# A decode-attention gradient kernel: K and V loads issued when four slots are free instead of three

## The chip, the cores and the metric

The kernel runs on one core of a Trainium2 chip. The metric is device microseconds for one execution: from three runs of the kernel before, a median of 731.6 us (lowest 729.88, highest 732.12).

## What is computed

The reference is one decode step (one token, width 640) of a layer with attention and a gated MLP side by side, forward and backward:

```python
xn = _layernorm(x)
# A: 32 heads of 128, each with its own K and V cache of 8192 x 128, bfloat16
q = (xn @ wq) ; scores = q k^T * 128**-0.5 ; p = softmax(scores) ; o = p v ; attention = o @ wo
# B: silu(xn @ w1) * (xn @ w3) @ w2, with 1728 hidden columns
out = x + attention + B
return out, and the gradients of <out, grad_out> for x, k_cache, v_cache, wq, wo, w1, w3, w2
```

With one query row, the gradients of the caches are outer products: dV is the softmax row times the gradient of o, dK is the gradient of the scores times q. So for each head the kernel reads K (2 MB) and V (2 MB) and writes dK (2 MB) and dV (2 MB). The page counts 151.34 MB read and 151.34 MB written.

## The kernel before

**Tiles and slots.** K or V of one head is one SBUF tile of 128 partitions x 8192 bfloat16 values, 2048 KB. There are ten such tiles (`NSLOT = 10`), named `kv` in the profile whatever they hold; the list `free_slots` is a first-in, first-out list of the free ones. Nothing is computed into a second tile: the outer products dV and dK are written by VectorE over the V and K that they belong to (L466), and the slot is stored to HBM from there.

**The order on the queue.** The schedule is written by hand. All K and V loads and all dK and dV stores are issued by SyncE (SP in the profile) through `fifo` (L105), in the order in which the program reaches them; SP waits in front of each one until what it needs is done, and everything behind it on SP waits too. Loads go K0, V0, K1, V1, ... and stores V0, K0, V1, K1, ... Each store is followed by an attempt to load:

```python
def load_next():
    if not pending or len(free_slots) < lag[0]:
        return
    ...
def store(kind, h):
    ...
    fifo((dkc if kind == "K" else dvc)[h], t[:])
    free_slots.append(t)
    load_next()
```

A slot counts as free in the program as soon as its store is issued. The load that takes it must wait on the chip until that store has landed. With `lag[0]` at 3, a load that follows a store takes the slot of the store two places earlier in the queue.

**The first heads.** Six loads (K0, V0, K1, V1, K2, V2) go out with `lag[0]` at 1; the other four slots (`mA` to `mD`) hold the MLP weights. Then `lag[0]` is set for the rest of the program (L160). Heads 0 and 1 follow; their stores are V0, K0, V1, K1. The MLP is computed ahead of head 2 (`MLP_AT = 2`), with its own stores issued by GpSimd (POOL); as each of its four slots is given back, `load_next` is tried again (L632, L666, L677).

**One head.** `head(h)` transposes K and V in eight pieces each (`T`, L318 on TensorE, L320 on ScalarE), multiplies them with q and with the gradient of o (`Mp`, L339), makes the softmax (`expo`, `zsum`, `probs`), and sums over K and V (`wsum`, L433). The outer products of head h-1 are made inside head h: `outers_a(h - 1)` at its start (all of dV with its store, half of dK), `outers_b(h - 1)` after `probs(h)` (the other half of dK, and its store). TensorE's first pieces of K of the next head are transposed before a head ends.

**Groups and the end.** Every four heads the weights wq and wo of a group are loaded by GpSimd and their gradients are stored, mostly by GpSimd. After head 31 come the last outer products, the gradients of the last group (`fin_wo` L520, `fin_wq` L526 and L528; their stores are split in two and go by SP, L515), and the input gradient (L843 to L865). Four small stores of the two output rows are issued by ScalarE (L849, L867). SP's last store of dwq waits until one of these small stores has landed.

Of the kernel before, what the change touches and what calls it, by code (L numbers as in the profile page):

```python
# [21 lines left out]
def kernel(  # L22
# [97 lines left out]
    lag = [1]  # L120
# [36 lines left out]
    for _ in range(2):  # L157
        load_next()

    lag[0] = 3  # L160

    ident_f = consts.tile([P, P], F32, name="ident_f")
    make_identity(nc, ident_f[:])
# [734 lines left out]
```

## Time and profile before

| what | value |
|---|---|
| median of the runs | 731.6 us |
| span of the profiled execution | 727.5 us |
| around the span (median less span; the page gives no other total of that execution) | 4.1 us |
| moved by DMA | 303.54 MB, 417 GB/s over the span |
| TensorE matmul busy | 603.3 us (83%) |
| VectorE busy | 459.8 us (63%) |
| ScalarE busy | 376.2 us (52%) |
| GpSimd busy | 32.3 us (4%) |

Busy times are sums over one execution and overlap each other. The DMA figures are a mean over the core's 16 DMA engines; a transfer of a K or V tile is spread over all 16 in 128 packets of 16 KB, and it has landed when the last engine is done with its share. The chain of work that ended last is followed back from the last instruction, and its shares say what was waited for, not what was busy.

### The profile page before, as it was taken

The page shows a single profiled execution, that of the slowest core. Times are in us where ns is not written, and L with a number is a line of the kernel's source. Part 1 is how long each engine was busy: PE and PEld are TensorE (multiplying, and loading weights), DVE is VectorE, ACT ScalarE, POOL GpSimd, SP SyncE. Part 2 cuts the span into 40 slices and gives each one's busy share as a digit, 9 for nine tenths or more (in the row PEclk, how much of TensorE's full clock was granted, in tenths as well). Part 3 has the DMA queues.
Part 4 walks back from the last instruction along what each step waited for, and adds up shares of the span by engine and source line. Part 5 has one row for each costly group of instructions (what it writes and reads, how often), then busy time and mean ns, then how long its engine had stood idle before and what let it go on. Part 6 is the DMA issues. An engine that isn't in the chain of part 4 may idle for free.

```text
span 727.5 us, 12942 instructions
## 1 busy us (share of the span) xinstructions
PE 603.3 (83%) x5186; PEld 377.1 (52%) x5193; DVE 459.8 (63%) x811; ACT 376.2 (52%) x727; POOL 32.3 (4%) x48
## 2 busy tenths in 40 slices
PE   4989489999899989888897789878796988988930
PEld 2547366665565556555454456445554555545510
DVE  4169646688868776667565756457665666667581
ACT  3640746665666566545454546455463555655510
POOL 0010100000000000000010000000000000000000
PEclk9997799999999999989998989899998999999965
DMA  9999999999999999999999999999999999999995
GB/s 351 400 411 421 428 426 430 427 426 430 420 420 431 430 412 420 426 428 421 420 425 428 430 426 428 420 431 428 421 422 427 429 425 423 425 432 427 426 415 221
DMA packets 28625, 303.54 MB, mean 417 GB/s; under 512 B 3354, under 2 KB 5929, under 8 KB 11924
## 3 DMA queue, kind: packets, MB, share of 16 engines
q1 hardware_dynamic: 22578, 277.75, 90.5%
q0 software_dynamic: 5968, 24.94, 8.5%
q8 instruction: 41, 0.67, 0.4%
q14 instruction: 20, 0.16, 0.1%
q10 hardware_dynamic: 18, 0.01, 0.0%
HBM read 151.34 MB, written 151.34 MB: 416 GB/s over the span
## 4 chain that ended last, share of the span: by engine, by line
DMA 51%; PE 36%; DVE 7%; ACT 2%; issue 1%; SPq 0%; ACTq 0%; DVEq 0%
DMA kv<-in_A_v_cache_dram 20%; PE pT L318 17%; DMA out_dram<-kv 16%; DMA kv<-in_A_k_cache_dram 14%; PE sA L339 5%; PE dA L339 4%; PE X L433 3%; DVE kv L466 3%; PE m L356 2%; DMA wo_g<-in_A_wo_dram 2%; ACT KT L320 1%; PE gu_ps L561 1%; PE pT L266 1%; PE m L400 1%; ACT KT L346 0%
## 5 line engine op out<-in xcount | busy, mean ns | idle before, releaser
L320 ACT COPY KT<-pT 128x512 f32<-128x512 f32 x512 | 288.3, 588 | 227.9 <-PE pT L318 208.6
L318 PE MATMUL pT<-ident_f,kv 128*128 128x128 f32 x2048 | 308.2, 290 | 53.7 <-DMA kv<-in_A_v_cache_dram 24.2
L318 PEld LDWEIGHTS pT<-ident_f,kv 128*128 128x128 f32 x2048 | 237.4, 149 | 146.2 <-PE pT L318 51.8
L466 DVE TENSOR_TENSOR kv<-qd,U 128x4096 bf16<-128x4096 bf16 x64 | 146.0, 2284 | 0.0
L466 DVE TENSOR_TENSOR kv<-qd,P 128x4096 bf16<-128x4096 bf16 x64 | 143.6, 2285 | 0.0
L433 PE MATMUL X<-kv,Z 128*32 128x512 bf16 x1024 | 97.1, 413 | 1.8 <-DVE Z L450 1.8
L339 PE MATMUL dA<-KT,qz 128*32 128x512 bf16 x512 | 84.2, 408 | 0.0
L339 PE MATMUL sA<-KT,qz 128*32 128x512 bf16 x512 | 83.5, 406 | 0.0
L416 DVE SCALAR_TENSOR_TENSOR U<-m,P 128x64 bf16<-128x64 f32 x32 | 7.5, 233 | 87.4 <-PE m L356 87.4
L433 PEld LDWEIGHTS <-Z 128*32 128x32 bf16 x1024 | 33.2, 101 | 35.3 <-issue 8.7
L339 PEld LDWEIGHTS <-qz 128*32 128x32 bf16 x1024 | 29.5, 95 | 40.8 <-issue 38.3
L382 DVE TENSOR_REDUCE mrow<-m 128x1 f32<-128x64 f32 x32 | 7.1, 223 | 68.4 <-PE m L356 68.3
L356 PE MATMUL m<-selc,KT 64*128 64x64 f32 x256 | 30.5, 242 | 10.3 <-ACT KT L346 10.3
L356 PEld LDWEIGHTS m<-selc,KT 64*128 64x128 f32 x256 | 21.5, 144 | 33.2 <-ACT KT L346 22.1
L376 ACT CAST qd<-pT 128x256 bf16<-128x256 f32 x32 | 11.9, 372 | 39.9 <-DVE kv L466 28.7
L389 DVE TENSOR_REDUCE negM<-m 128x1 f32<-128x128 f32 x32 | 9.3, 292 | 33.0 <-PE m L386 33.0
L526 DVE SCALAR_TENSOR_TENSOR wq_g<-wq_g,side 128x512 bf16<-128x512 bf16 x40 | 27.3, 683 | 0.0
L257 DVE SCALAR_TENSOR_TENSOR side<-wo_g,g_bc 128x640 bf16<-128x640 bf16 x32 | 26.2, 819 | 1.3 <-DMA wo_g<-in_A_wo_dram 0.9
L448 DVE SCALAR_TENSOR_TENSOR U<-m,P 128x128 bf16<-128x128 f32 x32 | 11.4, 356 | 16.3 <-PE m L446 16.3
L406 DVE RECIPROCAL rZ<-m 128x1 f32<-128x1 f32 x32 | 5.3, 166 | 24.2 <-PE m L400 24.2
L346 ACT COPY KT<-dA 64x512 f32<-64x512 f32 x32 | 18.6, 582 | 3.7 <-PE dA L339 3.7
L346 ACT COPY KT<-sA 64x512 f32<-64x512 f32 x32 | 18.6, 581 | 2.1 <-PE sA L339 1.9
(162 smaller groups left out, 372.7 us busy)
## 6 DMA issues: line engine op xcount, KB each, us to landing
out_dram<-kv SPq DMA_DIRECT2D x64, 2048.0 KB
kv<-in_A_k_cache_dram SPq DMA_DIRECT2D x32, 2048.0 KB
kv<-in_A_v_cache_dram SPq DMA_DIRECT2D x32, 2048.0 KB
wq_g<-in_A_wq_dram POOLq DMA_DIRECT2D x7, 640.0 KB, 13.4
wo_g<-in_A_wo_dram POOLq DMA_DIRECT2D x7, 640.0 KB, 19.1
out_dram<-wo_g POOLq DMA_DIRECT2D x7, 640.0 KB, 14.4
kv<-in_B_w_dram SPq DMA_DIRECT2D x2, 1728.0 KB
out_dram<-kv POOLq DMA_DIRECT2D x2, 1728.0 KB, 23.5
```

The costliest lines, as they stand in the source:

```text
L257: nc.vector.scalar_tensor_tensor(junk[:], G_["wo"][:, hh, :], 1.0, g_bc[:], ALU.mult, ALU.mult, accum_out=G_["do"][:, hh:hh + 1])
L318: nc.tensor.transpose(pT[:, k * P:(k + 1) * P], W3[:, 4 * c + k, :], ident_f[:])
L320: nc.scalar.copy(KT[:].rearrange("p k w -> p (k w)"), pT[:])
L339: nc.tensor.matmul(S_[kind][q:q + QW, :], lhsT=S_["qz"][:, o:o + QW], rhs=KTb[c][:, par, :], start=(c0 == 0 and par == 0), stop=(c0 == NCH ...
L346: nc.scalar.copy(XS[0:QH].rearrange("p k w -> p (k w)"), S_.pop(kind)[0:QH, :])
L356: nc.tensor.matmul(S_["m"][:, b0:b0 + 4 * J].rearrange("p (x c k t) -> p k x c t", x=4, k=4, t=2)[:, k], lhsT=XS[0:QH, k, :], rhs=selc[0:Q ...
L376: nc.scalar.copy(qd[:].rearrange("p a d -> p (a d)"), hd[h].pop("ps_r"))
L389: nc.vector.tensor_reduce(S_["negM"][:], S_["m"][:, 2 * J:2 * J + P], AX.X, ALU.max, negate=True)
L433: nc.tensor.matmul(xg["X"][q:q + QW, :], lhsT=Z[:, o:o + QW], rhs=W[:, N4 * i:N4 * (i + 1)], start=(slot == 0 and i < 4), stop=(slot == NS ...
L448: nc.vector.scalar_tensor_tensor(S_["U2"][:], S_["V"][:, 0:J].unsqueeze(2).to_broadcast([P, J, 2]), S_["m"][:, OC + NS:OC + NS + 1], S_["P ...
L466: nc.vector.tensor_tensor(dst[:, lo * DH:hi * DH].rearrange("p (j a b) -> p j a b", a=DH // 2, b=2), vec.rearrange("p (a b) -> p a b", b=2 ...
L526: nc.vector.scalar_tensor_tensor(wq_g[:, ci, :], wq_g[:, ci, :], 1.0, dqb, ALU.mult, ALU.mult, accum_out=dxa[:, ci, g:g + 1])
```

## The change

After the six first loads, `load_next` asks for four free slots instead of three.

```diff
     for _ in range(2):
         load_next()
 
-    lag[0] = 3
+    lag[0] = 4
```

The instructions of TensorE, VectorE, ScalarE and GpSimd stay as they are, in the same order. On SP the same 148 rows stand in another order. K3 no longer precedes the store of K1 but follows it; V3, K4, V4 and K5 follow it as before; V5 no longer precedes the store of V2 but follows it; and every later load stands behind one store more than before. The last load, V31, stood between the stores of K27 and V28 and now stands between those of V28 and K28. A load that follows a store takes the slot of the store three places earlier in the queue instead of two.

## The prediction

> **What bounds the kernel now.** I read the page's slices first, then stretches of the span, SP's own waits and issues, and the chain at the end. The slices show no stage after the first in which the transfers rest:
>
> ```profile
> DMA  9999999999999999999999999999999999999995
> GB/s 351 400 411 421 428 426 430 427 426 430 420 420 431 430 412 420 426 428 421 420 425 428 430 426 428 420 431 428 421 422 427 429 425 423 425 432 427 426 415 221
> ```
>
> Stretches (start and end, length, busy time of PE, weight loads, DVE, ACT and POOL, then granted clock, busy share of the DMA engines, GB/s) show the same where this change acts:
>
> ```profile
> 110.00:120.00 10.00, 10.00 (x100) 6.25 (x100) 6.29 (x12) 6.01 (x13) 0.00 (x0) 1.00 1.01 430
> 120.00:130.00 10.00, 9.41 (x76) 5.89 (x74) 8.62 (x17) 6.90 (x16) 0.00 (x0) 1.00 1.00 424
> ...
> 300.00:657.00 357.00, 303.98 (x2511) 187.25 (x2515) 219.47 (x370) 187.80 (x373) 14.60 (x18) 0.92 1.01 426
> ...
> 690.00:700.00 10.00, 5.13 (x55) 2.64 (x54) 9.27 (x10) 1.92 (x5) 0.00 (x0) 0.85 0.99 419
> 700.00:705.00 5.00, 1.81 (x12) 0.88 (x12) 3.88 (x8) 0.59 (x1) 0.00 (x0) 0.50 0.95 403
> 705.00:710.00 5.00, 0.00 (x0) 0.00 (x0) 4.82 (x17) 0.00 (x0) 0.00 (x0) 0.50 1.00 426
> 710.00:715.00 5.00, 0.93 (x3) 0.59 (x3) 2.24 (x12) 0.00 (x0) 0.00 (x0) 0.50 0.82 325
> 715.00:720.00 5.00, 0.00 (x0) 0.00 (x0) 0.00 (x0) 0.00 (x0) 0.00 (x0) 0.50 0.80 284
> 720.00:727.50 7.50, 0.00 (x0) 0.00 (x0) 0.00 (x0) 0.00 (x0) 0.00 (x0) 0.50 0.26 92
> ```
>
> All 16 DMA engines are busy from 10 us to about 690 us, and still mostly busy after the last outer product. PE is not the bound: 304 of 357 us in the long middle stretch. So the kernel runs at the rate of its transfers, and the order of two transfers in the queue costs time only where an engine of the 16 runs out of work. SP's waits look alarming, and are only the other face of this:
>
> ```profile
> SPq L105 <- DMA out_dram<-kv: 470.8, 55, 14.7
> SPq L105 <- DVE kv L466: 83.4, 13, 12.9
> ```
>
> SP stands 471 us in front of loads whose slot is still being stored; while it stands, up to four earlier transfers are under way.
>
> **The change part by part.** No byte, no instruction of an engine and no duration changes: a 2.097 MB tile at the 426 GB/s of the middle stretch is 4.92 us of all 16 engines, before and after. What moves is each load's place, by one store.
>
> *The middle, 130 to 650 us.* The load into a slot waits for the store three places back, not two, so up to six transfers may be under way instead of four. SP's wait moves to the stores. For the second half of dK of head h, VectorE needs `probs(h+1)`, and that comes behind pieces of V(h+1) on TensorE. At the end of the trace V31 lands at 683.3 and VectorE begins that half of dK30 at 690.2, done at 692.5: 9.2 us after the landing. With the new order the load of V(h+1) stands two transfers ahead of the store whose landing releases SP, so SP comes to the store of dK(h) about 4.9 us after V(h+1) landed and waits some 4.3 us for VectorE. Behind that wait stand only loads. What covers it is the queue: seven transfers (34 us of work) were issued behind the landed one. They do not finish evenly: the completion events of the load V31 run from 665.4 on the fastest of the 16 engines to 683.3 on the slowest, 18 us, which leaves the fastest engine about 16 us of work. I cost the middle at 0. Without that cover the 4.3 us would recur per head, some 25 times.
>
> PE's waits for loads (46.7 us in all on L318 in the trace) stay as many: K and V arrive one store later, but at the same rate. Here the Trainium skill speaks against the change: "DMA: Bandwidth & Descriptors", section "Rules for kernel authors", says to issue a DMA early and wait on it late. By that rule a later load is a loss, and taken at its word for V31 it makes the sum 4.9 us longer; in the middle, the rows above say that bytes alone set the pace. The same page's "Specifications" give about 358 GB/s as a core's limit for HBM; the trace holds 426 for 357 us, so the measurement decides, and by the page one tile would be an estimated 5.9 us.
>
> *Behind the MLP, 92 to 130 us.* Here a store moves ahead of a load where VectorE is late. SP's issues before:
>
> ```profile
> 92.75 0.96 SPq L105 DMA_DIRECT2D kv<-in_A_k_cache_dram  x1
> 107.20 0.33 SPq L105 DMA_DIRECT2D kv<-in_A_v_cache_dram  x1
> 120.41 0.34 SPq L105 DMA_DIRECT2D out_dram<-kv  x1
> 124.47 0.33 SPq L105 DMA_DIRECT2D kv<-in_A_k_cache_dram  x1
> 129.68 0.34 SPq L105 DMA_DIRECT2D out_dram<-kv  x1
> ```
>
> The load at 107.20 is V5; the store at 120.41 is dV2, which waited 12.9 us for VectorE (the longest of the waits on L466). After the change V5 stands behind dV2 and is issued at about 120.8. Until then the engines live on K5 and on POOL's MLP stores, the last of which was issued at 98.3 and landed 29.7 us later, at 128.0. dV2 landed between 128.6 and 132.2 on the 16 engines, median 130.1; less its own 4.9 us, the engines were free for it at 123.7 to 127.3, median 125.2. Without V5 they are free 4.9 us sooner: 118.8 to 122.4, median 120.3. A transfer issued at 120.4 reaches the engines about 1 us later (a store of dwo at the end: issued 709.14, first packet 710.10). So the fastest engine rests 2.6 us, the median one 1.1 us, the slowest not at all. The end is set by engines that are late, so the cost lies between 0 and 2.6 us; I take 0.6, nearer to the slow ones. The next pair then comes at 129.7 instead of a load at 124.5 and a store at 129.7; dV2 and V5 keep the engines until 131.2 or later, and the new packets start at 130.7. No second gap, but a margin of only 0.5 us.
>
> *Before that, 57 to 92 us,* dK1 is issued when VectorE is done with it (61.6 us; the row of its outer product starts at 57.12 and lasts 4.49) instead of at 66.71 behind K3. The engines are full in both orders, and K3 is needed only from about 98 us: 0.
>
> *The end.* This is the place where the later load can show. The chain of waits there:
>
> ```profile
> 657.53 25.79 DMA kv<-in_A_v_cache_dram
> ...
> 698.30 4.48 DVE kv L466 x2
> ...
> 713.40 0.28 DVE fin_bf L865
> ```
>
> V31 lands at 683.3; dK31 is done 19.5 us later at 702.8, and the last result of all, `fin_bf`, at 713.7. With one more store ahead of it, V31 lands 4.9 us later, at 688.2, and all of that chain moves by 4.9: dV31 done at 703.3, dK31 at 707.7, `fin_bf` at 718.6. Does the end move? The completion events of the last stores on the slowest engine follow at 4.9 to 6.3 us without a break: 709.1, 713.9, 718.7 and for dK31 723.6. There dK31, issued at 704.3, did not start before 718.7: 14.4 us of slack, of which the change uses 3.4. The two pieces of the slowest engine behind it (dwo, dwq) need their data by 710.2 and 715.2 instead of 705.3 and 710.3, still ahead of 723.6. What does depend on the chain is SP's last store, 340 KB of dwq on few engines, issued at 721.1 when ScalarE's small store of `fin_bf` had landed. That one was issued at 713.7 and its packets ran only at 719.4 to 720.6, behind the dwo part that was issued at 712.1. After the change the dwo part is issued at about 717.1. Its 272 packets (68 partitions, four rows each) are 55 ns each and run on four engines, 68 on each, 3.7 us: from 718 to 722. Then `fin_bf` has landed between 719.9 and 722.2, and the last store goes out between 1.1 us sooner and 1.1 us later than now. I take +0.4; if it keeps its present distance to `fin_bf`, all 4.9.
>
> **Sum.** 0 + 0.6 + 0 + 0 + 0.4 = +1.0 us: a span of 728.5 against 727.5. The runs' median stands 4.1 us above the span, so 732.6 against 731.6.
>
> **Rivals.**
> - *The end is not covered (slower).* ScalarE's last small store runs 7.4 us after its issue, as now, so that SP's last store is issued at 726.0 and the end moves by the whole 4.9 us. With the 0.6 of the gap: 737.1. It decides if the delay of the small store belongs to its issue and not to the dwo part ahead of it; for it speaks that SP's wait for it is 5.4 us long now, against it that its packets ran beside the last of that part. A part of it is enough for a slowdown from 2 us on.
> - *The gap behind the MLP is whole (slower).* If the engines that rest at 119 us are those that end last, or VectorE brings dV2 or dK2 later, up to one load's worth is lost: 4.9 + 0.4, 736.9. Against it: the backlog of 3.3 to 6.9 us behind 120.4.
> - *A deeper queue feeds the engines better (faster).* If the middle has small rests that six transfers in flight fill, it may rise from 426 to the 430 of the best slices: 1% of 357 us, 3.4 us, less the 1.0: 729.2, or 728.2 without the losses. Against it: the busy share there is 1.01.
> - *Nothing of it acts.* SP's rows do change order and the waits with them, so this would mean only that all is hidden: 731.6, inside the likeliest case.
>
> **How the numbers follow.** A difference of 0.3% (2.2 us) is about what a measurement of this kernel can tell from no change. The covered case is the likeliest, with 0.62: its gap of 0 to 2.6 and its end of -1.1 to +1.1 make -1.1 to +3.7, 730.5 to 735.3; of the 0.62, 0.10 lies above +2.2. The uncovered end has 0.22, the whole gap 0.06, the better-fed engines 0.10. So faster 0.10, same 0.52, slower 0.10 + 0.22 + 0.06 = 0.38. Leaving out the faster rival and what both slower ones together would cost, the range is 729.6 to 737.1.
>
> **What would show it.** In the changed profile: a middle stretch at 425 to 427 GB/s; V5 issued at 120.8; SP waiting far longer for L466 than 83 us and less for stores; a short dip of the DMA share at 119 to 122 us; V31 landing near 688; SP's last store near 721 to 722. I am wrong if V31 lands more than 7 us later (the gap was whole, or the middle slowed), if the middle changes its rate, or if the last store is issued near 726.

## The result, and the profile after

The changed kernel takes 737.91 us (median of 4 runs, 736.33 to 738.78) against 731.4 for the kernel before on the same chip (4 runs): a ratio of 1.0096, with an interval of 1.0077 to 1.0114. A second measurement with other runs of both gave 737.19 against 730.57, 1.0096 again (1.007 to 1.0122). The medians differ by 6.5 us (7.0 by the ratio), where +1.0 was forecast, and the time lies just above the range.

The profiled execution of the changed kernel has a span of 735.7 us and a time of 737.54, so 1.8 us lie around the span. The execution of the kernel before that the prediction was summed on, 727.5 us of span, was thus a quick one, some 2 us below its median; of the 8.2 us between the two spans, about 2 are this choice of executions.

The slices of the page now show a stage in which the transfers rest (the seventh, 110 to 129 us, where the busy share falls one tenth and the rate by a quarter), and behind it a slow slice at 129 to 147 us (396 GB/s) in which the engines are busy:

```profile
DMA  9999998999999999999999999999999999999995
GB/s 355 399 409 423 429 430 322 396 424 422 419 415 428 430 412 425 423 430 425 426 423 428 428 424 421 423 428 430 421 424 422 429 426 415 429 426 429 427 399 205
```

Stretches of the same profile, with the columns as in the prediction (the last three are granted clock, DMA busy share and GB/s):

```profile
110.00:115.00 5.00, 5.00 (x41) 3.19 (x37) 1.96 (x8) 3.78 (x9) 0.00 (x0) 1.00 1.00 423
115.00:120.00 5.00, 5.00 (x60) 2.91 (x59) 2.41 (x5) 2.57 (x5) 0.00 (x0) 1.00 0.87 363
120.00:125.00 5.00, 5.00 (x41) 3.17 (x40) 5.00 (x4) 3.63 (x7) 0.00 (x0) 1.00 0.40 166
125.00:130.00 5.00, 5.00 (x39) 3.09 (x37) 3.69 (x13) 3.30 (x8) 0.00 (x0) 1.00 0.97 347
...
140.00:145.00 5.00, 5.00 (x41) 3.14 (x40) 3.02 (x3) 3.72 (x8) 0.00 (x0) 1.00 1.00 360
...
300.00:657.00 357.00, 302.47 (x2532) 184.38 (x2533) 219.74 (x359) 187.46 (x370) 15.02 (x19) 0.93 1.01 425
...
720.00:730.00 10.00, 0.93 (x3) 0.59 (x3) 3.14 (x15) 0.00 (x0) 0.00 (x0) 0.50 0.66 231
```

Three things are to be seen. At 115 to 130 us the engines rest for 0.13 x 5 + 0.60 x 5 + 0.03 x 5 = 3.8 us; the packet records of 100 to 150 us give 3.96 us of rest per engine, and 0.0 before. At 140 to 145 us the engines are fully busy and still move only 360 GB/s. The middle is what it was: 425 against 426.

SP's issues (start, us, what) say why the engines rest, and where the end lies:

```profile
91.12 0.33 SPq L105 DMA_DIRECT2D kv<-in_A_k_cache_dram  x1
122.81 0.34 SPq L105 DMA_DIRECT2D out_dram<-kv  x1
123.25 0.58 SPq L105 DMA_DIRECT2D kv<-in_A_v_cache_dram  x1
132.07 0.34 SPq L105 DMA_DIRECT2D out_dram<-kv  x1
...
716.28 3.04 SPq L105 DMA_DIRECT2D out_dram<-wo_g  x2
727.42 0.71 SPq L105 DMA_DIRECT2D out_dram<-wq_g  x2
```

After K5 at 91.12 SP issues nothing for 31 us. dV2 comes at 122.81, behind VectorE, and V5 behind it at 123.25 instead of 107.20. K5 has landed by 118.0 and the last store of the MLP between 118.9 and 121.6 on the 16 engines, and dV2's packets begin 0.84 us after its issue. SP's waits show the same stand as the longest one on L466 (total, times, longest):

```profile
SPq L105 <- DMA out_dram<-kv: 234.4, 48, 9.6
SPq L105 <- DVE kv L466: 222.3, 35, 31.3
```

The chain at the end (start, us, what):

```profile
658.89 35.36 DMA kv<-in_A_v_cache_dram
...
709.23 4.49 DVE kv L466 x2
...
724.33 0.28 DVE fin_bf L865
```

V31 lands at 694.25 instead of 683.3, 10.9 us later: the one store of 4.9, and 6.0 from upstream. The whole chain behind it moves by as much; `fin_bf` is done at 724.6. On the slowest engine the transfers are less late: dK31 ends there at 728.7 instead of 723.6, 5.1 us (on the quickest at 720.4 instead of 710.4, 10.0 us). But the two last dwq stores on SP, whose data were ready at 721.2, are issued at 727.42 and 727.80, and the last of them lands at 734.8. In front of them SP waits for ScalarE's small stores of the row `out_0` (tile `KT` in the profile; first what SP waited for, then ScalarE's issues):

```profile
SPq L105 <- DMA out_dram<-KT: 8.0, 1, 8.0
...
721.98 2.67 ACTq L849 DMA_DIRECT2D out_dram<-KT  x2
```

These small stores and the dwq stores behind them use the same two completion semaphores in the trace.

### The profile page after: what moved, and what is told of

Read it like the earlier page. It is cut to its first block, busy times and chain, and to the rows that moved or that the text cites. A ratio compares the mean times of both kernels' runs of the same rounds, so it can differ in the third digit from the quotient of the medians.

```text
span 735.7 us, 12948 instructions
## 1 busy us (share of the span) xinstructions
PE 605.8 (82%) x5193; PEld 376.8 (51%) x5193; DVE 459.7 (62%) x811; ACT 376.5 (51%) x727; POOL 32.3 (4%) x48
## 4 chain that ended last, share of the span: by engine, by line
DMA 53%; PE 33%; DVE 8%; ACT 3%; issue 1%; SPq 0%; ACTq 0%; DVEq 0%
DMA kv<-in_A_v_cache_dram 20%; DMA kv<-in_A_k_cache_dram 16%; PE pT L318 16%; DMA out_dram<-kv 15%; PE sA L339 4%; DVE kv L466 4%; PE dA L339 3%; PE X L433 3%; PE m L356 2%; DMA wo_g<-in_A_wo_dram 2%; ACT kv L642 1%; ACT KT L320 1%; PE gu_ps L561 1%; PE dh_ps L572 1%; PE dx_acc L660 1%
## 5 line engine op out<-in xcount | busy, mean ns | idle before, releaser
L318 PE MATMUL pT<-ident_f,kv 128*128 128x128 f32 x2048 | 305.8, 288 | 65.0 <-DMA kv<-in_A_k_cache_dram 41.5
L318 PEld LDWEIGHTS pT<-ident_f,kv 128*128 128x128 f32 x2048 | 235.2, 148 | 157.5 <-issue 59.7
L466 DVE TENSOR_TENSOR kv<-qd,U 128x4096 bf16<-128x4096 bf16 x64 | 146.0, 2284 | 0.0
L466 DVE TENSOR_TENSOR kv<-qd,P 128x4096 bf16<-128x4096 bf16 x64 | 143.6, 2284 | 0.0
L433 PE MATMUL X<-kv,Z 128*32 128x512 bf16 x1024 | 100.9, 426 | 1.8 <-DVE Z L450 1.8
```

Source lines behind the costliest of these rows:

```text
L318: nc.tensor.transpose(pT[:, k * P:(k + 1) * P], W3[:, 4 * c + k, :], ident_f[:])
L433: nc.tensor.matmul(xg["X"][q:q + QW, :], lhsT=Z[:, o:o + QW], rhs=W[:, N4 * i:N4 * (i + 1)], start=(slot == 0 and i < 4), stop=(slot == NS ...
L466: nc.vector.tensor_tensor(dst[:, lo * DH:hi * DH].rearrange("p (j a b) -> p j a b", a=DH // 2, b=2), vec.rearrange("p (a b) -> p a b", b=2 ...
```

## The experiments

**Theory A (two places).** The main cost is the gap behind the MLP: the engines run dry because V5 stands behind dV2, and dV2 waits for VectorE. A smaller one is the end, where V31 comes one store later. **Theory B:** nearly all of it is the end; the gap is made up by late engines as the prediction had it. **Theory C:** the deeper queue costs something per head. The middle's 425 GB/s already spoke against C.

**1. Only the end.** The three slots stay until head 16; from there it is four.

```diff
     for h in range(H):
+        if h == 16:
+            lag[0] = 4
```

> Four free slots are asked for only from head 16 on; up to there three, as before. V5 keeps its place ahead of dV2, V31 stands behind one store more. Theory A (the engines ran dry behind the MLP, and that is most of the 6.5 us; the end adds some 1 to 3): +1 to +3 us against the kernel before, V31 landing about 4.9 us later than the 683 of before, no dip of the DMA share near 120 us. Theory B (the later last load is what costs, at the end): +5 to +7 us. Theory C (the middle runs slower with loads issued later): about half, +3 to +4, with a rate under 425 GB/s after 360 us only.

Measured: 732.35 us against 730.76 (12 and 24 runs), ratio 1.0019 (1.0002 to 1.0037): 1.4 us by the ratio. No rest at 100 to 150 us (0.01 us). The middle from head 16 on and the end together are worth about a fifth of the loss, so C and B both fall as the main cause. Its last two dwq stores show the same wait as in the changed kernel: VectorE is done with them at 717.2, and SP issues them at 723.1.

```profile
723.10 0.71 SPq L105 DMA_DIRECT2D out_dram<-wq_g  x2
```

**2. Only the gap.** Four slots until head 16, then three and one load more, so that V31 stands where it stood before.

```diff
-    lag[0] = 3
+    lag[0] = 4
...
+        if h == 16:
+            lag[0] = 3
+            load_next()
```

> Four free slots up to head 16, then three again, with one extra load issued there, so that V31 stands where it stood before. Theory A: +4.5 to +6 us, the dip of the DMA share near 120 us as with the change. Theory B: 0 to +1 us. Theory C: +3 to +4 us.

Measured: 735.2 us (7 runs) against 730.76, ratio 1.0055 (1.0034 to 1.0075): 4.0 us, the larger part, a little under the 4.5 to 6 expected. The profiled execution was the quickest of its seven (731.16, span 729.4), and it shows why they spread. There dV2 was issued at 118.87 instead of 122.81, and the rest is almost gone:

```profile
115.00:120.00 5.00, 5.00 (x48) 3.06 (x42) 5.00 (x3) 2.56 (x5) 0.00 (x0) 1.00 0.97 398
120.00:125.00 5.00, 5.00 (x40) 3.14 (x37) 3.79 (x8) 3.95 (x10) 0.00 (x0) 1.00 1.02 394
...
135.00:140.00 5.00, 5.00 (x42) 3.69 (x40) 3.87 (x2) 3.40 (x7) 0.00 (x0) 1.00 1.02 387
```

0.34 us of rest per engine, and yet 387 GB/s at full share: packets took longer here too (see the last section).

**3. The end's wait for the small stores.** The four small stores of the output rows go by GpSimd instead of ScalarE; once with the change (rows4), once with the kernel before (rows3).

```diff
-        nc.scalar.dma_start(out_0v[e:e + 1], ...)
+        nc.gpsimd.dma_start(out_0v[e:e + 1], ...)
...
-        nc.scalar.dma_start(out_1.rearrange(...)[lo:hi, :], fin_bf[lo:hi, :])
+        nc.gpsimd.dma_start(out_1.rearrange(...)[lo:hi, :], fin_bf[lo:hi, :])
```

> The change as it is (four slots throughout), but the four small stores of the two output rows at the end are issued by GpSimd instead of ScalarE, so that SP's last stores of dwq don't share their completion semaphores. If SP's wait for these small stores carries the end (the two dwq stores issued at 727.4 and 727.8 in the changed profile, dwq data being ready at 721.2): the dwq stores go out at 720 to 722, the end follows the slowest engine's dK31 (728.7) by about 3 us, and the time is 2.5 to 4 us below the changed kernel, +2.5 to +4 us against before. If the end follows the engines' backlog alone: as the changed kernel, +6 to +7.

> The kernel before, with the four small stores of the output rows issued by GpSimd. If the wait for them carries the end of the kernel before too (last dwq store issued at 721.1, data ready at 710.3): 1 to 2 us faster than before. If the slowest engine's dK31, landed at 723.6, sets the end there: within 0.5 us of before.

Measured: rows4 734.6 us, ratio 1.0056 (1.004 to 1.0072); rows3 729.09, ratio 0.9975 (0.9959 to 0.999), both against 730.76. In rows4 SP issues the two dwq stores when VectorE has made them, not 6 us later:

```profile
720.80 2.67 SPq L105 DMA_DIRECT2D out_dram<-wq_g  x2
```

So the wait for the small stores costs about 3 us in the changed kernel (737.2 and 737.9, less 734.6; by the ratios, 1.0096 less 1.0056, 2.9 us) and 1.7 us in the kernel before. Some 1 to 1.5 us of the change's loss go through that wait; 5.5 us between rows4 and rows3 do not, and the rest of 3.55 us behind the MLP is still there in rows4.

**4. dV2 earlier.** In the MLP the products of w3 over blocks of 256 columns, and their sums into the input gradient, are left out (line 654 runs over w1 alone), so that VectorE and TensorE are done with the MLP sooner; the kernel leaves out that part of the input gradient. Once with the change (less4), once without (less3).

```diff
-            for f0 in range(0, F, FA):
+            for f0 in range(0, F if wi == 0 else 0, FA):
```

> The changed kernel (four slots), with one piece of the MLP left out: of the input gradient's sum over w3 the part over the first four column blocks (seven products on VectorE, their sums on TensorE) isn't computed, which takes some 5 us of VectorE out of the stretch ahead of dV2. The transfers stay as they are. Theory A (the engines run dry because dV2, which now stands in front of V5, waits for compute): dV2 is issued at 116 to 118 us instead of 122.8, the engines run dry for 0 to 1 us instead of about 4, and the time is about that of the same kernel with three slots plus what the end costs: +1 to +2.5 us over that one. Without theory A: +6 us over that one, as before.

> The kernel before (three slots) with the same piece of the MLP left out. The engines are full around 120 us, so less compute there buys nothing: within 1 us of before. If compute ahead of head 3 sets the time: 4 to 5 us faster.

Measured: less4 732.54 us, ratio 1.0032 (1.002 to 1.0043); less3 729.46, ratio 0.9985 (0.9973 to 0.9997), against 730.18 (21 runs). In less4, dV2 and V5 are issued 6.4 us earlier than in the changed kernel:

```profile
116.36 0.34 SPq L105 DMA_DIRECT2D out_dram<-kv  x1
116.81 1.19 SPq L105 DMA_DIRECT2D kv<-in_A_v_cache_dram  x1
```

The rest is 0.01 us, packets keep their length, and the slowest engine ends dK31 at 723.1, where it did before. Between the two kernels with the shorter MLP the change costs 3.1 us, instead of 6.5. So with the gap closed, what is left is the end; it is larger here than the 1.4 us of late4 and than the 1 to 2.5 expected, with intervals that just meet. SP's last store of dwq is issued at 724.05 in less4 and at 720.96 in less3, 3.1 us later, as much as the time: in less4 the loss passes through the wait for the small stores.

**5. One slot more, one slot less.** If a place in the queue is what counts, five slots must be worse again, and two must move loads ahead.

```diff
-    lag[0] = 3
+    lag[0] = 5     (lag5)
+    lag[0] = 2     (lagtwo)
```

> Five free slots instead of three: K5 too stands behind dV2 (V5 behind dK2), and V31 two stores later than before. Theory A: the engines have one load less still and run dry for 8 to 9 us before dV2 arrives, with slower packets after it; with the end +11 to +16 us. Theory B or C (the later last load, the smaller lead alone, in proportion): about twice the change, +11 to +14, but without a longer dip near 120 us.

> Two free slots instead of three: every load one store earlier, V31 between the stores of V27 and K27; a load waits for the store just ahead of the last one, so only some three transfers are under way. If engines run dry in the middle because fast engines catch up with so short a queue: slower than before, +2 to +10 us, with a share under 1.00 from 300 to 657 us. If the queue of three is enough: the end gains, 0 to 2 us faster. SP's K6 now stands in front of dV2 and waits for an MLP store until about 124.5 us, which may add a gap of its own.

Measured: lag5 743.92 us, ratio 1.019 (1.0169 to 1.0212); lagtwo 733.48, ratio 1.0052 (1.0032 to 1.0071), against 730.18. In lag5 the engines stand still for nearly five microseconds, 6.0 us of rest in all, and its middle runs at 426 GB/s:

```profile
115.00:120.00 5.00, 5.00 (x48) 2.76 (x47) 4.96 (x5) 2.96 (x6) 0.00 (x0) 1.00 0.06 22
```

The rest is shorter than the 8 to 9 us expected. Rest and longer packets make about 8 of its 13.7 us. At 657 us its packets have moved what the kernel before had moved 8.4 us sooner, and its span ends 13.7 us later, so the remainder arises at the end, where V31 lands at 700.5, 17.2 us later; how it arises there was not followed further. lagtwo is slower too, mostly in the same stage but by another wait:

```profile
125.34 0.33 SPq L105 DMA_DIRECT2D kv<-in_A_k_cache_dram  x1
125.72 0.42 SPq L105 DMA_DIRECT2D out_dram<-kv  x1
```

Now K6 stands ahead of dV2 and waits until a store of the MLP has landed in its slot, so dV2, which VectorE had finished at 120.05, goes out at 125.7; the engines rest 1.5 us. Its middle moves 424 GB/s instead of 426, about 1.5 us in 357 us, with the busy share still at 1.01. In the stage behind the MLP three slots are right because V5 is ahead of dV2 and K6 behind it.

**6. The change behind the MLP, or from head 16 on, with the rows on GpSimd.** rowspost4 sets four slots from head 3 on, so that V5 stays ahead of dV2; rowslate4 does it from head 16; rows3b repeats rows3 beside them.

```diff
+        if h == 3:      (rowspost4; 16 in rowslate4; absent in rows3b)
+            lag[0] = 4
...
-        nc.scalar.dma_start(...)      (the small stores, as in 3)
+        nc.gpsimd.dma_start(...)
```

> Four free slots from head 3 on, that is just behind the MLP: V5 keeps its place ahead of dV2, and K6 and every later load stands behind one store more, as with the change. The small stores of the output rows are issued by GpSimd. So the middle runs with the changed order, and the two places that theory A names are both repaired. Theory A: as the three-slot kernel with the rows on GpSimd, within 2 us (-1.7 to +0.5 us against before); a small rest near 130 us may cost up to 1.5 us, since K6 now follows dK2. If the later loads cost anything in the middle, or V31's later landing at the end by itself: +3 to +6 us over that kernel.

> Four free slots from head 16 on, small stores of the output rows issued by GpSimd. The end alone, with its wait removed: 0 to +0.5 us over the three-slot kernel with the rows on GpSimd if SP's wait for the small stores is the end's whole price; +1.5 to +3 us over it if V31's later landing delays the end in another way.

> The three-slot kernel with the rows on GpSimd once more, as the comparison on the same chip: -1.7 us against before, between -3 and -0.5.

Measured, against 730.93 (25 runs): rowspost4 733.26, ratio 1.0044 (1.0026 to 1.0062); rowslate4 730.89, ratio 1.0012 (0.9994 to 1.003); rows3b 729.29, ratio 0.998 (0.9964 to 0.9996). rowspost4 is 4.0 us slower than rows3b, where theory A had at most 2 us and a costly middle or end +3 to +6; its profile says where:

```profile
119.96 9.63 SPq L105 DMA_DIRECT2D out_dram<-kv  x2
129.63 0.43 SPq L105 DMA_DIRECT2D kv<-in_A_k_cache_dram  x1
```

dV2 finds V5 ahead of it, but the next store, dK2 at 129.25, now stands ahead of K6 at 129.63, where K6 stood at 124.47 before. The gap has moved by one pair: 0.67 us of rest, and again longer packets. It is not the middle: compared with the kernel before at the same bytes moved, the profile is 2.8 us late at 165 us and 2.9 us at 300 and again at 657 us. rowslate4 is 1.6 us slower than rows3b although the small stores hold nothing up: at 690 to 700 us its engines have too little to do (rowslate4 first, then rows3b):

```profile
690.00:700.00 10.00, 9.72 (x73) 5.40 (x71) 3.60 (x8) 5.86 (x12) 0.00 (x0) 0.84 0.75 320
```

```profile
690.00:700.00 10.00, 5.49 (x54) 3.17 (x48) 9.30 (x8) 1.68 (x4) 0.00 (x0) 0.78 0.98 419
```

The stores of dV31 and dK31 cannot be made before V31 is there (it lands at 688.9 in rowslate4 and at 683.0 in rows3b), and no load is left to fill that time. The intervals of the two ratios meet, so the 1.6 us agree with late4's 1.4 and are no sharper than these.

**7. The change again.** The changed kernel a second time.

```diff
-    lag[0] = 3
+    lag[0] = 4
```

> The changed kernel once more, for a second profile and more runs. Theory A, with the engines free for dV2 at 119 to 122 us whatever the run, and dV2 issued between 118.9 and 122.8 us by the clock that TensorE was granted: +5 to +7.5 us in the median, runs spread over 3 us or more, and a dip whose length goes with the issue of dV2 in this profile (about 4 us of rest at 122.8, under 1 us below 119.5). If the dip has another cause, its length doesn't follow that time.

Measured: 737.19 us (6 runs, 737.01 to 739.08), the ratio given above. Its profile has the dip in the same place. In the four profiles with V5 behind dV2 and the whole MLP, the rest goes with the issue of dV2: 0.34 us at 118.87 (early4), 2.94 us at 122.07 (here), 3.55 us at 122.58 (rows4) and 3.96 us at 122.81 (the first profile). A stretch of this one:

```profile
120.00:125.00 5.00, 5.00 (x40) 3.14 (x38) 4.99 (x4) 3.88 (x8) 0.00 (x0) 1.00 0.57 229
```

The best version of all is rows3: three slots, and the small stores off ScalarE's queue, 0.9975 and 0.998 of the kernel before in two measurements.

## Why the prediction was wrong, point by point

**Behind the MLP: forecast 0.6 us in a span of 0 to 2.6, measured about 4.** This is the step that failed. Three parts of it did.
- *When dV2 comes.* The step took 120.4 us from one profile as if it were fixed. It is the end of a chain through the MLP on TensorE and VectorE, and over the kernels that keep the whole MLP dV2 was issued between 118.87 and 122.81 (lagtwo apart, where K6 stands ahead of it). The kernel before hides this, since V5 is under way while SP waits; the change turns it into rest of the engines almost microsecond for microsecond (3.6 us of rest more for 3.9 us of delay between early4 and the first profile), and the quickest and the slowest run of early4 lie 5 us apart. With the engines free at 118.8 to 122.4 as forecast and dV2 at 122.81 plus 0.84, the step's own sum gives a rest of 1.2 to 4.9 us instead of 0 to 2.6. The row at 120.41 was the reading of one execution, and its spread belonged into the range.
- *That late engines set the end.* I took 0.6 because the engines that end late would not rest. In the changed profile all of them rested (for 1.55 us no packet ran on any engine), and behind the rest they ran in step: dV2's completion events on the 16 engines lie within 0.6 us (129.4 to 130.0) instead of 3.6. A rest of all engines is lost to all.
- *Longer packets.* About 2 us more per engine were lost at 115 to 165 us in packets that took longer. The rows of before, where the engines do not rest there, did not show it.

The rival "the gap is whole" had this mechanism, VectorE bringing dV2 later, at 4.9 us, and 0.06. It was the nearest of the cases, in part by luck: its 4.9 us held neither the longer packets nor the 1.4 us of the end.

**The end: forecast +0.4, measured +1.4 to +1.6 alone (3.1 between less4 and less3).** The order of events was forecast rightly (V31 4.9 us later in itself, cover by the late stores), the size was not. The estimate let the dwo part run from 718 to 722 and the small stores land by 722.2. In the changed kernel the small stores of `out_0` were issued at 721.98 and 722.26 behind the dwo part of 719.04 and landed at 727.35 and 727.52, after 5.3 to 5.4 us instead of the 1.1 to 1.3 of the kernel before, where they were issued ahead of that part (711.04 and 711.32 against 712.14), and SP's last stores waited for them. So the rival "the end is not covered" had the right wait and roughly the right issue (726.0 forecast, 727.80 measured), but only 1 to 1.5 us of the loss pass through it; rowslate4 lost 1.6 us without it, by engines that had too little to do at 690 to 700. "Rules for kernel authors" in the Trainium skill's "DMA: Bandwidth & Descriptors", on issuing early, pointed the right way here; the 4.9 us that the prediction drew from it for V31 was too much.

**Around the span: 4.1 us taken, 1.8 measured.** The median minus one span mixes two executions. It hid that this profile was a quick one.

**The sum.** By the ratios, the gap alone (4.0) and the end alone (1.4) make 5.4 of 7.0 us. The remainder is within the intervals. The changed profile itself, compared with the kernel before at the same bytes moved, is 0.2 us early at 115 us, 5.9 us late at 150, 6.4 at 300 and 6.7 at 657, and its span ends 8.2 us later: in this execution the stage behind the MLP cost some 6 us, the middle next to nothing and the end 1.5. The reference is one execution (rows3, with three slots too, stands up to 2 us off it), so the standstill between 300 and 657 says more than each figure. Part of the remainder may be that a chain that is 10.9 us late and a backlog that is only 5.1 us late meet at the small stores. That part is argued, not shown.

**What was right.** The middle costs nothing: 425 GB/s over 357 us, although SP there waited 15 times for L466, 60.8 us in all, 4.1 us each where 4.3 was forecast. Nothing recurs per head. The stage of 57 to 92 us cost nothing (full share at 50 to 110 us). The better-fed engines did not appear: the rate had no rest to fill. PE's waits for loads on L318 did not stay as many (64.5 us instead of 46.7), which cost nothing, since the transfers set the pace. And two of the signs named beforehand came true, V31 more than 7 us later (10.9) and the last store near 726 (727.80).

## What to carry to other kernels

In this kernel, whose transfer engines are busy all the time, moving a load behind a store cost nothing in the steady middle (425 against 426 GB/s). In such a kernel look for the few places where the backlog is thin, at a change of phase and at the end, and ask there which transfer is still in the queue while the next one waits for an engine. The moment at which such a wait ends is one execution's reading: take its spread from several runs, since a load that was issued early may be hiding it. A small store on another queue can hold a large one up if someone waits for it, so it belongs where nothing large stands ahead of it.

## What the runs showed of the hardware

**Packets took longer after the engines had rested.** A packet of 16 KB takes 611 ns at the median in the profile before, and in the changed kernel too. But of those that start at 135 to 150 us in the changed kernel, 13% took more than 700 ns (up to 1.4 us), against 1.3% before. Summed over 115 to 165 us, the time above 611 ns is 2.2 us per engine, against 0.3 before; it is 1.9 to 2.4 us in every other kernel here whose engines rested between 0.3 and 6 us behind the MLP (early4, rows4, rowspost4, lag5, lagtwo, after2, the second profile of the change), and 0.3 to 1.0 in those without a rest (late4, less3, less4, rows3, rows3b, rowslate4). Where there was a rest, the packets behind it cost about 2 us more, however short it was. That the engines run in step then, and ask for the same thing at the same time, is seen beside it; that it is the cause was not tried.

**The time at which dV2 is ready went with the granted clock and with the start of the MLP.** From the first product of the MLP (L561) to the end of dV2's outer product it took 64.8 us in early4, where the mean granted clock at 50 to 110 us was 0.83; 64.8 to 66.2 in before, rowspost4 and rowslate4 at 0.80; and 66.3 to 67.8 in after, after2, late4, rows3, rows3b and lag5 at 0.77 (rows4, at 0.74, took 67.4). That first product began between 52.2 us (lag5) and 56.5 us (after), which goes with dV2 being issued at 119.88 in the one and at 122.81 in the other at the same clock. What sets that start was not followed. The kernels that run this stage with three slots show the same spread (64.8 to 67.8 us), so the change is not needed for it.
